# Batch 2's scores in two 64-row bursts, its u turned by DMA: one batch more on the later batches' path, in an attention and MLP-mixer kernel

## The chip, the cores and the metric

The kernel runs on one core of a Trainium2 chip. The metric is the device time of one execution in microseconds (us). A program orders the work of five engines: TensorE (PE, matmuls and their weight loads), VectorE (DVE), ScalarE (ACT), GpSimd (POOL) and SyncE (SP, which only issues DMAs here). Each engine works through its own list of instructions in order; between engines there are semaphores.

## The reference

Eight batches, eight heads, 576 positions, 64 numbers per head. Heads 0 to 3 attend to the last 32 positions, heads 4 to 7 to every fourth of the last 128. The result is a 576 x 512 matrix per batch, which an MLP mixer treats first across positions (token mix) and then across channels.

```python
rel = pos[:, None] - pos[None, :]
mask_plain = (rel >= 0) & (rel < window)                     # window 32, heads 0..3
mask_dil = (rel >= 0) & (rel < window * dilation) & (rel % dilation == 0)   # dilation 4, heads 4..7
attn = softmax(where(mask, q @ k.T / 8, -1e9))
x = (attn @ v), heads side by side                           # [8, 576, 512]
xt = x.transpose(0, 2, 1)
u = x + (np.maximum(xt @ w_tok1, 0.0) @ w_tok2).transpose(0, 2, 1)
out = u + np.maximum(u @ w_ch1, 0.0) @ w_ch2                 # 512 -> 1536 -> 512
```

## The kernel before, in words

**Stages of a batch.** Loads in fp32; casts to fp16 (`cast_steps`, L274, 9 for q, k and tails, 8 for v); q and k turned so that the 64 numbers of a head lie on partitions; scores and their exponentials; masks; `values` (L543), attention weights by v, with a column of ones for the sum, and DVE's reciprocal and product `xn`; the token mix `emit_h1` (L570) and `emit_u` (L581), whose sum with x is u; u turned (`emit_uT`, L607, on TensorE, or `uT_dma` and `uT_place`, L633 and L641, by DMA); and `gen_main` (L695), the channel MLP: twelve blocks `gp` of four 128x512 matmuls with a relu each, in odd batches also three blocks `gt` of the 64-row tails of two batches, then the products `yp` back to 512 channels, 24 matmuls of 256 columns for each quarter of the positions, added to u on DVE and stored.

**The order of the work.** The order is written by hand. `interleave` (L764) runs `gen_main(b)` piece by piece, counting an assumed time, and between the pieces puts the steps of later batches whose time has come: each step is a triple of time, cost and function. In the main part of batch b lie the values and the token mix of batch b+1, the scores and casts of batch b+2, and the loads of batch b+3. The tables of times are at the end of the program (L953 on), with a case of their own for b = 0, for b = 1, and one for all others. A step that issues instructions appends them to several engines' lists at once: a score step gives matmuls to PE, exponentials to ACT and masks to POOL.

**Two ways to make scores.** Batches 0 to 2 (`scores_plain`, `scores_dil`, L420 and L446) use all 128 rows of the array: the keys of two heads lie on 128 partitions, and the queries are copied into `qz`, padded with zeros for the other head. TensorE turns q and k there (`transposes`, L303) into one bank of PSUM per pair of heads. Batches 0 and 1 add a bias (`veil`) by a matmul; batch 2 is masked on POOL as the later ones are. Batches 3 to 7 (`by_dma`, L342) have q, k and tails turned by DMA into `qt`, `kr` and `tt`, unpadded; POOL copies the keys of the plain heads into `kt` (`place_steps`); and `scores_twin` (L465) issues two bursts, g = 0 for the plain heads and g = 1 for the dilated ones, each 24 matmuls over 64 rows, two heads at a time in the two halves of the array. A burst fills six banks: two of the ring `sc` and two of the ring `fl` for the four large tiles, one more of `fl` and one of `main` for the small ones (the last blocks and the tails of the 64 last positions). Behind it come its exponentials on ACT, eight for g = 0 (four of 480 columns, four of 256) and six for g = 1, and three masks on POOL. The ring `fl` has three banks and also serves the transposes, the values and the token mix.

**u.** For b < 3 (`turned`, L630) u is turned by 16 transposes on TensorE and copied out of PSUM by ACT and DVE. For b >= 3 it goes by DMA into `utm`; two of its four blocks are then copied by ACT into `utd`, in the order that `gen_main` wants.

**Start.** `warm(8)` (L779, L836) gives PE eight matmuls on zeros, into a bank that nobody reads, while the first loads travel. The first load of batch 2 waits for the second of three transfers of `w4` (`gate`, L803; q, k and v of batch 2 follow in SP's list). Relus of the gp blocks lie on ACT but for every second one in batch 0 and blocks 1 and 5 in the other batches, which are on DVE; of the three tail relus the first is on DVE.

Of the kernel before, what the change touches and what calls it, by code (L numbers as in the profile page):

```python
# [16 lines left out]
S = 576  # L17
# [51 lines left out]
def kernel(  # L69
# [272 lines left out]
    def by_dma(b):  # L342
        return b >= 3

    def dma_steps(b):

        def turn_over(t, c):
            nc.sync.dma_start_transpose(out=t, in_=c)

        def half(t, nm, i):  # L350
            turn_over(t[:, 2 * i:2 * i + 2].rearrange("p a r m -> p (a r) m"),
                      c16[(b, nm)][:, 2 * i:2 * i + 2].rearrange("m a r h d -> m (a r h d)"))

# [4 lines left out]
        return steps  # L358

    def place_steps(b):  # L360

# [43 lines left out]
    def plain_blocks(hp):  # L405
        return attp[hp].rearrange("p h (b c) -> p h b c", c=PST)
# [58 lines left out]
    def scores_twin(b, g):  # L465

        tags = (("sc", 2), ("sc", 2), ("fl", 3), ("fl", 3), ("fl", 3), ("main", 3))
        ps = [bank(*tags[i], f"sc_{b}_{g}_{i}") for i in range(6)]
        small = ps[4:6]

        def twin(hp, banks, c, keys, queries):
            for h in range(2):
                rows = slice(64 * h, 64 * h + 64)
                n = c.stop - c.start
                nc.tensor.matmul(out=banks[h][:, c], lhsT=keys(rows), rhs=queries(rows), start=True, stop=True)  # L475
# [12 lines left out]
        for j in range(2):  # L488
            hp = 2 * g + j
            if g == 0:  # L490
                twin(hp, small, slice(256 + 128 * j, 384 + 128 * j),
                     lambda rows: kt[hp][rows, 384:512], lambda rows: qta[rows, hp, :, 96:128])
            for x in range(2):
                twin(hp, small, slice(128 * j + 64 * x, 128 * j + 64 * x + 64),
                     lambda rows: kt[hp][rows, 384 + 128 * x:512 + 128 * x], lambda rows: tta[rows, hp, 0:64])
        yield 0.87

        def exp(out, in_):
            nc.scalar.activation(out=out, in_=in_, func=AF.Exp, scale=0.125)  # L499

        def main(hp):
            for h in range(2):
                p = ps[2 * (hp % 2) + h]
                if g == 0:
                    exp(plain_blocks(hp)[:, h, 0:3, 0:BLK].rearrange("p b (m r) -> p b m r", r=4),
                        p[:, 0:3 * BLK].rearrange("p (b r m) -> p b m r", r=4, m=40))
                else:
                    exp(attd[hp - 2][:, h], p)

        def rest():  # L510
            for h in range(2):
                p = small[h]
                if g == 0:
                    exp(attpa[:, :, h, 3 * PST:3 * PST + 128].rearrange("p a (m r) -> p a m r", r=4),
                        p[:, 256:512].rearrange("p (a r m) -> p a m r", a=2, r=4))
                t = attt[:, 2 * g:2 * g + 2, h, 64:TW].rearrange("p a (x c) -> p a x c", c=128)[:, :, :, 0:64]
                exp(t, p[:, 0:256].rearrange("p (a x c) -> p a x c", x=2, c=64))
# [21 lines left out]
        if not g:  # L539
            mask(1)  # L540
        yield 0.0

# [85 lines left out]
        uT[(b, cb)] = (t[:, 128:640], t[:, 0:128]) if odd else (t, None)  # L628

    def turned(b):  # L630
        return b >= 3

    def uT_dma(b, tail):  # L633
        i = b % 2
# [12 lines left out]
            uT[(b, cb)] = (uTd[:, cb - 2], tail)  # L647
            nc.scalar.copy(out=natural(uTd[:, cb - 2]), in_=uTm[i][:, cb].rearrange("p r m -> p m r"))

    def score_steps(b, t0, dt, offs=(0.0, 0.7, 2.0), places=None):  # L650

        steps = []
        if by_dma(b):
            for g in range(2):
                for i, f in enumerate([scores_twin(b, g)] * 2):
                    steps.append((t0 + g * dt, 0.86 * (i == 0), lambda f=f: next(f)))
# [38 lines left out]
    def gen_main(b):  # L695
# [7 lines left out]
        def gp_tails(g):  # L703
            p = bank("main", 3, f"gt_{b}_{g}")
            for i in range(4):
                for cb in order:
                    nc.tensor.matmul(  # L707
                        out=p[:, 128 * i:128 * i + 128], lhsT=w3_block(cb, 4 * g + i), rhs=uT[(b, cb)][1],
                        start=(cb == order[0]), stop=(cb == order[-1]))
            relu(nc.scalar if g else nc.vector, gta[:, 4 * g:4 * g + 4, 512:640],  # L710
                 p.rearrange("p (i t) -> p i t", t=128))

        for mb in range(NMB):
            p = bank("main", 3, f"gp_{b}_{mb}")
            for i, cb in enumerate(order):
                nc.tensor.matmul(out=p, lhsT=w3_block(cb, mb), rhs=uT[(b, cb)][0], start=(i == 0), stop=(i == 3))  # L716
# [236 lines left out]
    for b in range(B):  # L953
        steps = []
        if b == 0:
# [7 lines left out]
            steps += score_steps(2, 0, 0, (0.0, 1.0, 2.6),  # L963
                                 ((31.0, 33.8), (33.0, 0), (0, 0), (0, 0)))[:7]
            steps += at(37.0, 0.0, [lambda: emit_loads_qk(3)])
        elif b == 1:
            late = score_steps(2, -4.3, 2.4, (0.0, 0.7, 1.6))
            va = value_steps(2, 4.2, 1.0)
            steps += late[7:] + va[:4] + [(9.6 + (0.0, 0.8, 2.8, 3.6)[i], c, f) for i, (_, c, f) in enumerate(va[4:])]
            steps += mix_steps(2, 10.8, 14.6, 17.2, 22.2)  # L970
            steps += score_steps(3, 25.2, 4.2) + at(9.0, 0.6, cast_steps(3))
            steps += at(6.0, 0.0, [lambda: load_v(3)]) + at(20.0, 0.9, load_steps(4))
            steps += at(15.0, 0.7, dma_steps(3)) + at(20.6, 0.4, place_steps(3))
        else:
            late = 2.4 * (b % 2)
            if b + 1 < B:
# [37 lines left out]
```

## Time and profile before

| | us |
|---|---|
| median of three runs | 290.72 |
| lowest, highest | 290.5, 291.42 |
| the profiled execution | 292.38 |
| its span, first to last instruction | 290.6 |
| PE busy in it | 279.4 |
| POOL, ACT, DVE busy in it | 165.7, 134.8, 133.3 |

The profiled execution took 1.8 us beside its span. Times within a trace are counted from the span's start. The granted clock is full in every slice of the page. A row of the timeline has start, length, engine, line, operation, what it writes and reads, shape and count; in brackets, the idle time of the engine before it and what ended it. A matmul's length there reaches from its issue to the modelled end of its pipeline, so that successive ones overlap.

### The profile page before, as it was taken

The numbers are of one execution on the slowest core, as the hardware profiler recorded it, in microseconds if no ns is written. First come the engines' busy times: TensorE is split into PE (matmuls) and PEld (weight loads), VectorE is DVE, ScalarE is ACT, GpSimd is POOL, SyncE is SP. The second block draws the span as 40 slices with busy tenths as digits, with TensorE's granted clock in tenths as the row PEclk, the third lists the DMA queues.
The fourth block names the chain that finished last, engine by engine and source line by source line (L and its number), as shares of the span: only waits on it lengthen the run. The fifth ranks groups of instructions, "written<-read, shape, count | busy, mean of one in ns | idle before, by whom it ended". The sixth has DMA issues, their size and how long they took to land.

```text
span 290.6 us, 7078 instructions
## 1 busy us (share of the span) xinstructions
PE 279.4 (96%) x2850; PEld 214.5 (74%) x2850; DVE 133.3 (46%) x279; ACT 134.8 (46%) x266; POOL 165.7 (57%) x227
## 2 busy tenths in 40 slices
PE   5799999999999999999999999999999999999995
PEld 2687676898676886688676986697776966896594
DVE  6677668456734237413741255415640264422022
ACT  2764673247564703565347615482356525224500
POOL 6980860475996499739962998469952930000000
PEclk9999999999999999999999999999999999999999
DMA  7999998993999986769896989399974220431023
GB/s 215 274 205 260 267 215 165 318 227 95 304 211 204 325 241 151 87 120 346 213 204 137 324 203 219 74 219 333 193 144 97 88 74 2 86 114 38 2 73 108
DMA packets 103472, 52.11 MB, mean 179 GB/s; under 512 B 71792, under 2 KB 102384, under 8 KB 103440
## 3 DMA queue, kind: packets, MB, share of 16 engines
q1 hardware_dynamic: 99200, 46.55, 65.5%
q0 software_dynamic: 2640, 3.94, 7.8%
q10 hardware_dynamic: 1600, 1.18, 1.4%
q8 instruction: 22, 0.36, 0.5%
q14 instruction: 10, 0.08, 0.1%
HBM read 37.07 MB, written 9.44 MB: 160 GB/s over the span
## 4 chain that ended last, share of the span: by engine, by line
PE 65%; ACT 0%; DVE 0%; issue 0%
PE yp L735 25%; PE gp L716 21%; PE h1p L578 3%; PE up L590 3%; PE gt L707 3%; PE yp L755 3%; PE sc L475 2%; PE h1p L576 1%; PE av L554 1%; PE av L559 1%; PE up L601 1%; PE av L552 1%; PE yq L735 0%; PE av L564 0%; PE av L562 0%; ACT h L106 0%
## 5 line engine op out<-in xcount | busy, mean ns | idle before, releaser
L735 PE MATMUL yp<-w,gt 128*128 128x256 f16 x756 | 87.4, 273 | 0.0
L735 PEld LDWEIGHTS <-gt 128*128 128x128 f16 x768 | 78.5, 106 | 6.3
L106 ACT ACTIVATE gt<-gp 128x512 f16<-128x512 f32 x76 | 45.4, 597 | 81.1 <-PE gp L716 80.6
L716 PEld LDWEIGHTS <-w 128*128 128x128 f16 x384 | 39.0, 114 | 19.6 <-issue 0.5
L745 DVE TENSOR_TENSOR o<-yp,u 128x512 f32<-128x512 f32 x31 | 21.4, 691 | 64.2 <-PE yp L735 58.3
L112 POOL TENSOR_TENSOR attp<-attp,const 128x1280 f16<-128x1280 f16 x12 | 31.4, 2613 | 32.1 <-ACT attp L499 28.5
L716 PE MATMUL gp<-utd,w 128*128 128x512 f16 x120 | 45.6, 380 | 0.0
L716 PE MATMUL gp<-utm,w 128*128 128x512 f16 x120 | 45.5, 379 | 0.0
L716 PE MATMUL gp<-uT,w 128*128 128x512 f16 x144 | 38.7, 379 | 0.0
L112 DVE TENSOR_TENSOR xn<-av,rec 128x320 f16<-128x320 f32 x64 | 31.4, 491 | 2.2
L112 POOL TENSOR_TENSOR attd<-attd,const 128x1024 f16<-128x1024 f16 x12 | 25.3, 2132 | 0.0
L596 DVE TENSOR_TENSOR u<-up,xn 128x512 f16<-128x512 f32 x26 | 17.9, 690 | 8.5 <-PE up L590 8.5
L102 POOL CAST c_q<-l_q 128x512 f16<-128x512 f32 x31 | 19.4, 631 | 3.9 <-DMA l_q<-in_q_dram 2.2
L102 POOL CAST c_k<-l_k 128x512 f16<-128x512 f32 x29 | 17.8, 617 | 2.0 <-PE up L590 1.0
L106 ACT ACTIVATE h<-h1p 128x256 f16<-128x256 f32 x29 | 11.1, 383 | 15.9 <-PE h1p L578 15.7
L567 DVE RECIPROCAL rec<-av 128x5 f32<-128x5 f32 x64 | 12.1, 189 | 13.0 <-PE av L564 12.8
L108 DVE TENSOR_SCALAR gt<-gp 128x512 f16<-128x512 f32 x20 | 13.7, 685 | 7.5 <-PE gp L716 7.1
L392 PEld LDWEIGHTS <-kt 128*128 128x128 f16 x144 | 12.4, 105 | 5.1 <-DVE kt L314 2.6
L366 POOL COPY kt<-kr 128x512 f16<-128x512 f16 x10 | 10.8, 1076 | 9.1 <-DMA kr<-c_k 9.1
L499 ACT ACTIVATE attp<-sc 128x480 f16<-128x480 f32 (+1 forms) x30 | 13.4, 528 | 3.0 <-PE sc L475 3.0
L112 POOL TENSOR_TENSOR attt<-attt,const 128x512 f16<-128x512 f16 (+1 forms) x14 | 14.3, 1019 | 0.0
L605 DVE TENSOR_TENSOR u16t<-up,xn 64x512 f16<-64x512 f32 x7 | 4.8, 689 | 19.6 <-PE up L601 19.6
(136 smaller groups left out, 483.3 us busy)
## 6 DMA issues: line engine op xcount, KB each, us to landing
out_dram<-o SPq DMA_DIRECT2D x72, 128.0 KB, 3.0
l_q<-in_q_dram SPq DMA_DIRECT2D x15, 512.0 KB, 6.1
l_k<-in_k_dram SPq DMA_DIRECT2D x14, 512.0 KB, 7.1
l_vn<-in_v_dram SPq DMA_DIRECT2D x32, 128.0 KB, 6.3
l_vd<-in_v_dram SPq DMA_DIRECT2D x16, 256.0 KB, 5.2
w<-in_moe_w_ch_dram POOLq DMA_DIRECT2D x6, 512.0 KB, 7.6
lt<-in_q_dram SPq DMA_DIRECT2D x8, 128.0 KB, 3.7
l_vt<-in_v_dram SPq DMA_DIRECT2D x8, 128.0 KB, 5.4
```

Source lines behind the costliest of these rows:

```text
L102: eng.tensor_copy(out=out, in_=in_)
L106: nc.scalar.activation(out=out, in_=in_, func=AF.Relu)
L108: eng.tensor_scalar_max(out=out, in0=in_, scalar1=0.0)
L112: eng.tensor_tensor(out=out, in0=x, in1=y, op=ALU.mult)
L366: nc.gpsimd.tensor_copy(out=natural(kt[hp][:, 0:512]), in_=kra[:, hp].rearrange("p r m -> p m r"))
L392: nc.tensor.matmul(out=out, lhsT=lhsT, rhs=qz[hp][:, h, queries], start=hide is None, stop=True)
L499: nc.scalar.activation(out=out, in_=in_, func=AF.Exp, scale=0.125)
L567: nc.vector.reciprocal(out=rec[:, :, 0], in_=av[:, :, 64])
L596: nc.vector.tensor_tensor(out=u16(b, s), in0=blocks4(p), in1=blocks4(xn[b][:, s]), op=ALU.add)
L716: nc.tensor.matmul(out=p, lhsT=w3_block(cb, mb), rhs=uT[(b, cb)][0], start=(i == 0), stop=(i == 3))
L735: nc.tensor.matmul(out=p[:, c], lhsT=gta[:, mb, a0:m0 + 512:4] if half else gta[:, mb, a0:a0 + 128], rhs=w4[mb][:, c], start=(mb == 0), st ...
L745: nc.vector.tensor_tensor(out=blocks4(o32), in0=blocks4(p), in1=u16(b, s), op=ALU.add)
```

## The change

It does the following.

- Batch 2 uses `scores_twin` (`twinned`, b >= 2). As its data don't come by DMA, `bare_steps` turns tails, q and k on TensorE, without padding: one tile of four tail transposes (copied by DVE into `kt` and by ACT into `tt`), then per pair of heads a tile of q (copied by ACT into `qt`) and one of k (copied by DVE into `kt`, for the dilated heads into `kr` and a part into `kt`). The first five of these nine steps, the first burst, its exponentials and the other four steps lie in b = 0's main part, the second burst near the beginning of b = 1's.
- In all twins, of batches 2 to 7, the exponentials come in another order: the small tile of the ring `main` first, the four large ones, the small tile of the ring `fl` last. They are steps of their own. The masks stay in their order.
- Batch 2's u is turned by DMA (`turned`, b >= 2).
- In b = 1's main part nine of twelve relus are on DVE; batch 3's casts of q are on ACT; batch 2's values and mix and batch 3's scores come at later times (28.0 and 32.4 for the two bursts, 25.2 and 29.4 before); batch 4's loads too.
- All tail relus are on ACT.
- Nine warming matmuls instead of eight, and three more behind the first transposes.
- The first load of batch 2 waits for the first transfer of `w4` instead of the second.

```diff
+    def twinned(b):
+        return b >= 2
...
+    def bare_steps(b):
+
+        def tails():
+            p = bank("fl", 3, f"tp_t_{b}", FP16)
+            for hp in range(4):
+                nc.tensor.transpose(
+                    out=p[:, 128 * hp:128 * hp + 128],
+                    in_=c16[(b, "t")][:, 2 * hp:2 * hp + 2, :].rearrange("m h d -> m (h d)"), identity=ident)
+            t = p[:, 0:512].rearrange("p (x c) -> p x c", c=128)
+            nc.vector.tensor_copy(out=kta[:, :, 512:S], in_=t[:, :, 64:128])
+            nc.scalar.copy(out=tta, in_=t)
+
+        def turn_over(nm, hp):
+            p = bank("fl", 3, f"tp_{nm}_{b}_{hp}", FP16)
+            for r in range(4):
+                nc.tensor.transpose(
+                    out=p[:, 128 * r:128 * r + 128],
+                    in_=c16[(b, nm)][:, hp, r].rearrange("m h d -> m (h d)"), identity=ident)
+            grid = p[:, 0:512].rearrange("p (r m) -> p r m", r=4)
+            if nm == "q":
+                nc.scalar.copy(out=qta[:, hp], in_=grid)
+            elif hp < 2:
+                nc.vector.tensor_copy(out=natural(kt[hp][:, 0:512]), in_=grid.rearrange("p r m -> p m r"))
+            else:
+                nc.vector.tensor_copy(out=kra[:, hp], in_=grid)
+                nc.vector.tensor_copy(out=natural(kt[hp][:, 384:512]),
+                                      in_=grid[:, :, 96:128].rearrange("p r m -> p m r"))
...
-        main(2 * g)
-        if g:
-            mask(2)
-        main(2 * g + 1)
-        if g:
-            mask(3)
-        rest()
-        if not g:
+        yield from small_exps(1)
+        for hp in (2 * g, 2 * g + 1):
+            for h in range(2):
+                main(hp, h)
+                if g and h:
+                    mask(hp)
+                yield 0.0
+        yield from small_exps(0)
+        if g == 0:
             mask(0)
...
     def turned(b):
-        return b >= 3
+        return b >= 2
...
-            relu(nc.scalar if g else nc.vector, gta[:, 4 * g:4 * g + 4, 512:640],
+            relu(nc.scalar, gta[:, 4 * g:4 * g + 4, 512:640],
...
-            relu(nc.vector if (mb % 2 == 1 if b == 0 else mb in (1, 5)) else nc.scalar, gta[:, mb, m0:m0 + 512], p)
+            relu(nc.vector if (mb % 2 == 1 if b == 0 else mb % 4 != 3 if b == 1 else mb in (1, 5)) else nc.scalar, gta[:, mb, m0:m0 + 512], p)
...
-    warm(8)
+    warm(9)
...
     tp(0)
+    warm(3)
...
-    gate(l32[(2, "t")][0:1, 0, 0:1], w4[4][0:1, 0:1])
+    gate(l32[(2, "t")][0:1, 0, 0:1], w4[0][0:1, 0:1])
...
+            scores2 = score_steps(2, 33.2, 4.4, lag=0.2)
...
-            steps += score_steps(3, 25.2, 4.2) + at(9.0, 0.6, cast_steps(3))
+            steps += score_steps(3, 28.0, 4.4)
```

How the order moves at three places. The first is PE's list around batch 2's second transposes of k (`tp_k_2_1`; `sc_2_0` are the plain heads' score tiles, `yp_0_3` the last quarter of batch 0's output). Before:

```order
L392 MATMUL sc_2_0_0_1233<-qz_64,kt_65 128x160
L309 LDWEIGHTS c_k_2_1081
L309 MATMUL tp_k_2_1_1238<-const_61,c_k_2_1081 128x128
...
L735 LDWEIGHTS gt_93
L735 MATMUL yp_0_3_1225<-w4_87,gt_93 128x256
...
L392 LDWEIGHTS kt_65
L392 MATMUL sc_2_0_1_1250<-qz_64,kt_65 128x160
```

And now:

```order
L777 MATMUL yp_0_2_1156<-w4_87,gt_93 128x256
L378 LDWEIGHTS c_k_2_1086
L378 MATMUL tp_k_2_1_1222<-const_61,c_k_2_1086 128x128
...
L508 LDWEIGHTS kt_65
L508 MATMUL sc_2_0_0_1228<-qt_66,kt_65 128x160
...
L508 MATMUL sc_2_0_1_1229<-qt_66,kt_65 128x160
```

Before, single score groups stand between runs of six yp; now all 24 score matmuls follow the four transposes of k directly, one whole output quarter earlier in the list of yp.

The second is ACT's list from the end of batch 3's second burst on (`attd` and `attt` are weights of the dilated heads and of the tails, `gt_93<-gp_2_0` the first relu of batch 2's main part). Before:

```order
L499 ACTIVATE attd1_75<-sc_3_1_3_1841 128x512
L499 ACTIVATE attt_76<-sc_3_1_4_1842 128x2x2x64
L499 ACTIVATE attt_76<-sc_3_1_5_1843 128x2x2x64
L106 ACTIVATE gt_93<-gp_2_0_1969 128x512
L106 ACTIVATE gt_93<-gp_2_2_2023 128x512
```

And now:

```order
L532 ACTIVATE attt_76<-sc_3_0_4_1807 128x2x2x64
L532 ACTIVATE attt_76<-sc_3_1_5_1889 128x2x2x64
L532 ACTIVATE attd0_74<-sc_3_1_0_1884 128x512
...
L532 ACTIVATE attd1_75<-sc_3_1_3_1887 128x512
L532 ACTIVATE attt_76<-sc_3_1_4_1888 128x2x2x64
L687 COPY utd_92<-utm0_89 128x512 x2
L106 ACTIVATE gt_93<-gp_2_0_1944 128x512
```

The two copies of batch 2's turned u now stand between the exponentials and the relus.

The third is PE's list from batch 3's first burst (`sc_3_0`) on. Before, the burst's last matmul is followed by the whole of `yp_1_0` (the first quarter of batch 1's output) and the three quarters behind it:

```order
L475 MATMUL sc_3_0_5_1764<-tt_68,kt_65 128x64
L735 LDWEIGHTS gt_93
L735 MATMUL yp_1_0_1806<-w4_87,gt_93 128x256
...
L735 MATMUL yp_1_1_1878<-w4_87,gt_93 128x256
...
L735 MATMUL yp_1_2_1909<-w4_87,gt_93 128x256
...
L735 MATMUL yp_1_3_1938<-w4_87,gt_93 128x256
```

And now:

```order
L508 MATMUL sc_3_0_5_1808<-tt_68,kt_65 128x64
L777 LDWEIGHTS gt_93
L777 MATMUL yp_1_2_1795<-w4_87,gt_93 128x256
...
L777 MATMUL yp_1_3_1869<-w4_87,gt_93 128x256
...
L508 MATMUL sc_3_1_0_1884<-qt_66,kr_67 128x128
```

Before, all four quarters (96 matmuls) followed the burst; now 18 of the third and the whole fourth do, 42. The second burst lies among them in both.

More of the change, by code (lines that the diff above doesn't have):

```diff
@@ L358, in dma_steps @@
         return steps
+    def bare_steps(b):
[23 more added lines that the diff above has]
+                                      in_=grid[:, :, 96:128].rearrange("p r m -> p m r"))
+        return [tails] + [lambda nm=nm, hp=hp: turn_over(nm, hp) for hp in range(4) for nm in ("q", "k")]
     def place_steps(b):
@@ L499, in exp, with main, last_blocks, tails @@
             nc.scalar.activation(out=out, in_=in_, func=AF.Exp, scale=0.125)
[L501 to L517, printed above, removed]
+        def main(hp, h):
+            p = ps[2 * (hp % 2) + h]
+            if g == 0:
+                exp(plain_blocks(hp)[:, h, 0:3, 0:BLK].rearrange("p b (m r) -> p b m r", r=4),
+                    p[:, 0:3 * BLK].rearrange("p (b r m) -> p b m r", r=4, m=40))
+            else:
+                exp(attd[hp - 2][:, h], p)
+        def last_blocks(h):
+            exp(attpa[:, :, h, 3 * PST:3 * PST + 128].rearrange("p a (m r) -> p a m r", r=4),
+                small[h][:, 256:512].rearrange("p (a r m) -> p a m r", a=2, r=4))
+        def tails(h):
+            t = attt[:, 2 * g:2 * g + 2, h, 64:TW].rearrange("p a (x c) -> p a x c", c=128)[:, :, :, 0:64]
+            exp(t, small[h][:, 0:256].rearrange("p (a x c) -> p a x c", x=2, c=64))
         def mask(hp):
@@ L525, in mask, with small_exps @@
                 mult(nc.gpsimd, w, w, band[:, :, :, 0:128])
-        main(2 * g)
-        if g:
-            mask(2)
-        main(2 * g + 1)
-        if g:
-            mask(3)
-        rest()
-        if not g:
+        def small_exps(h):
+            if g == 0:
+                last_blocks(h)
+                yield 0.0
+            tails(h)
+            yield 0.0
+        yield from small_exps(1)
[4 more added lines that the diff above has]
+                    mask(hp)
+                yield 0.0
+        yield from small_exps(0)
+        if g == 0:
             mask(0)
@@ L538, in scores_twin @@
         mult(nc.gpsimd, t, t, tails_seen[g])
-        if not g:
+        if g == 0:
             mask(1)
@@ L648, in uT_place, with score_steps @@
             nc.scalar.copy(out=natural(uTd[:, cb - 2]), in_=uTm[i][:, cb].rearrange("p r m -> p m r"))
-    def score_steps(b, t0, dt, offs=(0.0, 0.7, 2.0), places=None):
+    def score_steps(b, t0, dt, offs=(0.0, 0.7, 2.0), places=None, lag=0.0):
         steps = []
-        if by_dma(b):
+        if twinned(b):
             for g in range(2):
-                for i, f in enumerate([scores_twin(b, g)] * 2):
-                    steps.append((t0 + g * dt, 0.86 * (i == 0), lambda f=f: next(f)))
+                f = scores_twin(b, g)
+                at = t0 + g * dt
+                steps.append((at, 0.86, lambda f=f: next(f)))
+                for i in range(7 if g else 9):
+                    steps.append((at + lag * (i + 1), 0.0, lambda f=f: next(f)))
             return steps
@@ L962 @@
             steps += at(24.0, 0.5, casts)
[L963 to L964 removed]
+            bare = bare_steps(2)
+            scores2 = score_steps(2, 33.2, 4.4, lag=0.2)
+            scores2 = sorted(scores2, key=lambda st: st[0])
+            steps += [(t, 0.25, f) for t, f in zip((30.2, 30.8, 31.4, 32.0, 32.6, 35.1, 35.5, 35.9, 36.3), bare)]
+            steps += scores2[:10]
             steps += at(37.0, 0.0, [lambda: emit_loads_qk(3)])
         elif b == 1:
[L967 to L970, printed above, removed]
[L971 to L973 removed]
+            va = value_steps(2, 7.0, 1.0)
+            steps += [(1.4 + 0.5 * i, c, f) for i, (_, c, f) in enumerate(scores2[10:])]
+            steps += va[:4] + [(13.4 + 0.9 * i, c, f) for i, (_, c, f) in enumerate(va[4:])]
+            steps += mix_steps(2, 12.4, 17.4, 20.4, 32.6)
+            casts = cast_steps(3)
+            steps += [(10.0 + 0.6 * i, 0.0, casts[i]) for i in (0, 2, 4, 6, 8)]
+            steps += [(10.0 + 1.2 * i, 0.0, lambda i=i: cast_qk(3, "q", i, nc.scalar)) for i in range(4)]
+            steps += at(17.0, 0.3, casts[9:])
+            steps += score_steps(3, 28.0, 4.4)
+            steps += at(6.0, 0.0, [lambda: load_v(3)]) + at(22.0, 0.9, load_steps(4))
+            steps += at(16.0, 0.7, dma_steps(3)) + at(20.6, 0.4, place_steps(3))
         else:
```

## The prediction

> **What bounds the kernel now.** I read the page's busy times first, then the timeline of TensorE (PE), then, at each place where the change puts something else, the timelines of ScalarE (ACT), VectorE (DVE) and GpSimd (POOL), and last the chain of waits.
>
> ```profile
> PE 279.4 (96%) x2850; PEld 214.5 (74%) x2850; DVE 133.3 (46%) x279; ACT 134.8 (46%) x266; POOL 165.7 (57%) x227
> ```
>
> PE is the bound on average: the other engines have 40% and more to spare. So the time changes by the PE work that is removed, and by the stalls of PE that come or go. Columns in what follows: start in us, length, engine, line, what; in brackets the idle time before it and its releaser. Lengths on PE are from issue to end, so I take the distance of starts as the cost of matmuls.
>
> Three landmarks: 61.45, where batch 1's third block of u has been transposed (up to there the order is the old one, but for the first 15 us); **T1**, the end of batch 3's first burst of scores (96.14 now); **L**, batch 3's first product of head 4 with its tails (112.09 now). Behind L the order is again the old one.
>
> ```profile
> 61.45 0.82 PE L735 MATMUL yp<-w,gt 128*128 128x256 f16 x6
> 65.13 0.37 PE L392 MATMUL sc<-qz,kt 128*128 128x160 f16 x3
> 65.33 0.39 PE L309 MATMUL tp_k<-const,c_k 128*128 128x128 f16 x4
> 65.56 0.82 PE L735 MATMUL yp<-w,gt 128*128 128x256 f16 x6
> 67.73 0.39 PE L392 MATMUL sm<-qz,kt 128*128 128x128 f16 x6
> 67.96 1.03 PE L716 MATMUL gp<-uT,w 128*128 128x512 f16 x4
> 71.98 0.39 PE L392 MATMUL sc<-qz,kt 128*128 128x128 f16 x4
> 72.20 0.39 PE L309 MATMUL tp_k<-const,c_k 128*128 128x128 f16 x4
> 75.20 0.20 PE L562 MATMUL av<-vv,attt 128*128 128x65 f16 x1 [0.24 <-POOL attt L112]
> ...
> 91.43 0.23 PE L624 MATMUL tpu<-const,u 128*128 128x128 f16 x1 [0.19 <-DVE u L596]
> ...
> 95.81 0.23 PE L475 MATMUL sc<-qt,kt 64*128 64x128 f16 x2 [0.37 <-DVE uT L102]
> 96.14 2.79 PE L735 MATMUL yp<-w,gt 128*128 128x256 f16 x24
> ...
> 99.54 8.04 PE L735 MATMUL yp<-w,gt 128*128 128x256 f16 x72
> 107.41 0.59 PE L716 MATMUL gp<-uT,w 128*128 128x512 f16 x2
> 112.09 0.19 PE L562 MATMUL av<-vt,attt 128*128 128x65 f16 x1
> ```
>
> The bracketed rows are the long waits of the old order here. Counted from issue to issue they are .41, .35 and .55, and gaps under .2 add about .5: 1.8 us that the old order loses between 61.45 and T1, and nothing from T1 to L.
>
> **Work taken off PE.** Batch 2's scores are four groups of 3 matmuls (65.13 to 65.33, .20), two of 6 (67.73 to 67.96, .23), four of 4 (71.98 to 72.20, .22), and two of four half as wide, which I estimate at .11: 2.36 us. The two bursts take their place:
>
> ```profile
> 124.80 0.75 PE sc L475 x24
> 128.93 0.67 PE sc L475 x24
> ```
>
> That is batch 4's pair, 1.42 us: .94 saved. The transposes of q and k stay on PE, with the tails in a tile of their own. Batch 2's u loses 16 transposes at .058 (four in .23, 65.33 to 65.56): .9. Together **-1.8**. The old stalls, which hung on that u and on the masks and scores at their old places, go too: **-1.8**.
>
> **New stalls before T1.**
>
> ```profile
> 61.65 0.69 ACT L100 COPY uT<-tpu 128x640 f16<-128x640 f16 x1 [1.18 <-PE tpu L626]
> ```
> ```profile
> 65.76 0.69 DVE L314 COPY kt<-tp_k 128x512 f16<-128x512 f16 x1 [0.60 <-PE tp_k L309]
> ```
> ```profile
> 95.33 2.23 ACT L499 ACTIVATE attp<-sc 128x480 f16<-128x480 f32 x5 [0.87 <-PE sc L475]
> 97.40 0.43 ACT L499 ACTIVATE attt<-sc 128x256 f16<-128x256 f32 x1
> 97.67 0.45 ACT L499 ACTIVATE attp<-sc 128x256 f16<-128x256 f32 x1
> 99.36 2.06 ACT L499 ACTIVATE attd<-sc 128x512 f16<-128x512 f32 x4 [0.97 <-PE sc L475]
> 101.28 0.69 ACT L499 ACTIVATE attt<-sc 128x256 f16<-128x256 f32 x2
> 131.80 2.13 ACT L648 COPY utd<-utm 128x512 f16<-128x512 f16 x2
> ```
>
> (1) Batch 1's last block of u now comes eight transposes (.44) after 61.45, in the PSUM bank that ACT copies out from 61.65 to 62.34; 61.89 becomes 62.40: .5. (2) The first burst stands right behind the last k transposes. DVE starts on such a copy .20 after them (65.56, 65.76), takes .69, and a PE waiting for it starts some .06 later: .95, of which six matmuls of the burst hide .20: .75. (3) The burst uses all three banks of the transposes' ring. Twelve yp (1.31) lie behind it, then q2, k2, q3, k3 want those banks back. ACT can begin .20 after the burst's end T, takes the small exps of the other bank first (2 x .27, 97.40 to 97.67), then the mains at .45 (95.33 to 97.40 holds four and one small). The third main ends near T+2.2, while PE is ready at T+1.3: .9; the next three banks cost .23, .41 and .21 in the same way: 1.8. (4) The token mix comes a little ahead of the last normalization on DVE, which now has nine of batch 1's twelve relus: .3, between 0 and 1. Sum **+3.4**; the lower end is 0 if the banks come free sooner than the exps' row says, the upper 4.5.
>
> **From T1 to L.** This is the main term. Now 96 yp (24 and 72) follow T1; in the new order 42 do, since batch 3's bursts stand 54 matmuls later. A yp costs .1093 (99.54 to 107.41 is 72 of them). PE's own work there is 42 x .1093 = 4.59, the second burst .67 and, from 107.41 to 112.09, 4.68: 9.94. Against it stands POOL, which masks what ACT has exponentiated:
>
> ```profile
> 98.26 2.61 POOL L112 TENSOR_TENSOR attp<-attp,const 128x1280 f16<-128x1280 f16 x1 [4.91 <-ACT attp L499]
> ...
> 108.69 1.15 POOL L112 TENSOR_TENSOR attt<-attt,const 128x512 f16<-128x512 f16 x1
> ```
>
> The masks run without a gap from 98.26 to 109.84: 11.58. In the new order the first one needs the last exp but one: T1 + .20 + 2 x .27 + 4 x .45 + .45, and .14 to POOL (97.67+.45 to 98.26) = T1 + 3.13. So L can't come before T1 + 14.71, and with .06 it is T1 + 14.77. PE is ready at T1 + 9.94: **+4.8** of stall. Now the masks end 2.25 ahead of L, so there it costs nothing. Part of the 4.8 is met sooner: the first gp of batch 2 waits for the copy of its turned u (131.80: two in 2.13), queued on ACT behind all exps of both bursts. The second burst ends at T1 + 3.95, its exps follow from T1 + 4.15 (.27, four at .48 by 99.36 to 101.28, .27), and the first copy ends near T1 + 7.7, where PE stood ready at T1 + 5.3. These 2.5 are inside the 4.8, not beside it.
>
> Sum: -1.8 - 1.8 + 3.4 + 4.8 = **+4.6** from 61.45 to L.
>
> **Start.** The warming matmuls are the part that can gain.
>
> ```profile
> 2.54 3.60 PE L783 MATMUL idle_p<-idle 128*128 128x512 f16 x8 [2.54 <-POOL idle L160]
> 6.77 0.59 PE L309 MATMUL tp_q<-const,c_q 128*128 128x128 f16 x4 [0.64 <-DMA const<-consts]
> ...
> 8.57 0.32 PE L392 MATMUL sc<-qz,kt 128*128 128x160 f16 x1 [0.65 <-ACT qz L100]
> ...
> 10.02 0.63 PE L309 MATMUL tp_q<-const,c_q 128*128 128x128 f16 x4
> 10.44 0.63 PE L309 MATMUL tp_k<-const,c_k 128*128 128x128 f16 x4
> ...
> 11.86 0.24 PE L392 MATMUL sc<-qz,kt 128*128 128x160 f16 x1 [0.24 <-DVE kt L314]
> ...
> 14.62 0.40 PE L309 MATMUL tp_k<-const,c_k 128*128 128x128 f16 x4 [0.68 <-DVE c_k L102]
> ```
> ```profile
> 8.43 0.52 DVE L102 CAST c_k<-l_k 128x512 f16<-128x512 f32 x1
> 11.11 0.69 DVE L314 COPY kt<-tp_k 128x512 f16<-128x512 f16 x1 [2.16 <-PE tp_k L309]
> ...
> 12.56 2.00 DVE L102 CAST c_k<-l_k 128x512 f16<-128x512 f32 x1
> ```
>
> Four transposes cost .42 at 10.02 and .23 at 65.33: PE runs at half rate until about 11, though it has worked since 2.54, with idle pieces of .64 and .65 between. One warming matmul more goes into the first, three into the second. If the full rate then comes near 8.5, the 1.45 from 8.57 to 10.02 and the .85 of the next eight transposes halve, DVE's copy at 11.11 comes 1.1 sooner, and the cast behind it, whose end PE awaits at 14.62, by up to as much; that cast takes 2.00 where the one on DVE at 8.43 takes .52, so a luckier place could give another 1.5. Bounds: -2.5 to +.5 (four matmuls at .45 by the row at 2.54, less the 1.29 that was idle). Batch 1's casts on POOL later absorb some. I take **-1.2**, half of the gain's end, since PE and DVE share the chain.
>
> The Trainium skill ("TensorE: Matmul & The Clock Gate", Part 1) says that the array is at half rate by default, goes to full after a busy window of some 3.4 us that runs freely, and so at a moment that varies from run to run. The rows agree on the half rate; that idle pieces of .64 kept the window from counting is not shown. By the rule alone the gain may be there in one run and not in another, which is the rival "cold start" below.
>
> **Edits with one answer.** Queries cast on ACT rather than POOL, batch 2's loads released by an earlier weight transfer, tail relus on ACT: taken as 0. They lie on engines at 46 to 57% while PE is the bound. The new order of exps delays the first mask of the later batches by .54 (two small exps):
>
> ```profile
> 138.56 1.16 POOL L112 TENSOR_TENSOR attt<-attt,const 128x512 f16<-128x512 f16 x1
> ```
> ```profile
> 140.79 0.19 PE L562 MATMUL av<-vt,attt 128*128 128x65 f16 x1
> ```
>
> Batch 4's masks end 139.72, 1.07 ahead of their use: .5 stays.
>
> **The number.** +4.6 - 1.2 = +3.4. The profiled execution lasted 292.38 us (span 290.6 and 1.8 around it); its like would be 295.8. It is 1.7 above the median of 290.72, so I forecast 290.72 + 3.4 = 294.1. About .3%, .87 us, is what can be told from no change.
>
> **Rivals.**
> - *Cold start.* The rate comes no sooner: the start gives 0 to +.5, and the sum is +4.6 to +5.1: 295.4. For it: PE was awake 8 us in vain. Against: the idle is there to be filled. Chance .22.
> - *The stalls before T1 don't come, the masks bind.* If ACT and DVE return the banks in time, T1 is 3.4 sooner: +1.2 without the start, 0.0 with it: 290.8 to 291.9. For it: the bank order is worked out by hand. Chance .12.
> - *Faster: the masks don't bind either.* If POOL's chain from T1 took less than 9.94, PE's work alone would decide: -1.8 - 1.8 - 1.2 and what is left of 3.4, that is -1.4 to -4.8; 288.5. It decides where 11.58 of masks fall below 6.8, so half of the first burst's masks must have been done earlier than I place them. Against it: they can't start before the burst. Chance .06. A start gain of 2.5 together with the second rival gives 289.5: .06.
> - *Worse: the loss carries on.* The 1.07 of batches 4 and 6 is used up because POOL goes behind L later by 2 us with casts, and each loses up to 1; or a stall of 2.5 us puts PE at half rate again, some 3 us at double cost, +1.5. No row shows a stall above .68 after 12 us. 297. Chance .07.
>
> The forecast keeps .47; its own range, with half to all of the 3.4 and the start from 0 to -2, is 292.0 to 295.3. From 290.2 to 296.0 leaves out most of the third rival and the last. Faster .12: the third and its neighbour; same .09: most of the second; slower .79.
>
> **What would show it.** Right: batch 3's first masks start about 3.1 behind the burst, PE waits for POOL at head 4's tails and for ACT's copy at batch 2's first gp, 4 to 5 us together; and three to four waits near 62 to 70 for ACT and DVE. The start: four transposes in .23 before 10. Wrong: PE without idle between T1 and L, or batch 3's burst near its old time.

## The result and the profile after

| | us |
|---|---|
| before, median of 4 (lowest, highest) | 290.61 (290.38, 291.42) |
| changed, median of 4 (lowest, highest) | 295.88 (295.08, 297.13) |
| ratio, 95% interval | 1.0163, 1.0129 to 1.0197 |
| profiled execution of the changed kernel, its span | 295.08, 293.2 |
| profiled execution of before, its span | 292.38, 290.6 |

The change costs 5.3 us by the medians, 4.7 by the ratio (3.7 to 5.7 by its interval). The two profiled executions differ by 2.7 only, and that is itself a finding: the one of before was 1.8 us slower than its median (experiments b0 and w1), and the one of the changed kernel was the fastest of its four.

The page of the changed kernel: busy times, and the row of the granted clock in 40 slices.

```profile
PE 279.2 (95%) x2838; PEld 211.8 (72%) x2838; DVE 132.5 (45%) x277; ACT 134.6 (46%) x266; POOL 163.3 (56%) x221
...
PEclk9999999999999998999999999999999999999999
```

PE is busy about as long as before in a span that is longer, although work was taken off; and one slice, the sixteenth (110 to 117 us), has a clock below the rest. TensorE's list of waits (what waited, for whom, us in total, how often, the longest):

```profile
PE gp L758 <- ACT utd L687: 3.3, 1, 3.3
...
PE tp_q L378 <- ACT attp L532: 0.8, 1, 0.8
...
PE sc L508 <- DVE kt L385: 0.5, 1, 0.5
...
PE tpu L654 <- ACT uT L100: 0.3, 1, 0.3
```

All four are new, and all four are waits that the prediction named. Here they are on TensorE's timeline, first those before batch 3's first burst. The place that was 61.45 is 59.64 now.

```profile
59.64 0.39 PE L368 MATMUL tp_t<-const,c_t 128*128 128x128 f16 x4
59.87 0.39 PE L378 MATMUL tp_q<-const,c_q 128*128 128x128 f16 x4
60.59 0.38 PE L654 MATMUL tpu<-const,u 128*128 128x128 f16 x4 [0.33 <-ACT uT L100]
...
62.94 0.38 PE L508 MATMUL sc<-qt,kt 64*128 64x160 f16 x6
63.79 0.44 PE L508 MATMUL sc<-qt,kt 64*128 64x160 f16 x8 [0.47 <-DVE kt L385]
...
64.33 1.50 PE L777 MATMUL yp<-w,gt 128*128 128x256 f16 x12
66.63 0.38 PE L378 MATMUL tp_q<-const,c_q 128*128 128x128 f16 x4 [0.79 <-ACT attp L532]
67.09 0.38 PE L378 MATMUL tp_k<-const,c_k 128*128 128x128 f16 x4
67.64 0.38 PE L378 MATMUL tp_q<-const,c_q 128*128 128x128 f16 x4 [0.17 <-ACT attt L532]
68.12 0.38 PE L378 MATMUL tp_k<-const,c_k 128*128 128x128 f16 x4
68.34 2.13 PE L777 MATMUL yp<-w,gt 128*128 128x256 f16 x18
```

Bracketed idle times are short because the pipeline still drains; counted from issue to issue, the last block of u comes .50 late (60.09 to 60.59), the second half of the burst .6, and the four late transposes, .22 each when nothing holds them, take from 65.64 (12 yp behind 64.33) to 68.34: 1.8 of waiting. Now the boundary between batches 1 and 2, on TensorE, ScalarE, GpSimd and SyncE:

```profile
100.00 3.45 PE L777 MATMUL yp<-w,gt 128*128 128x256 f16 x30
...
104.05 1.50 PE L777 MATMUL yp<-w,gt 128*128 128x256 f16 x12
108.84 0.38 PE L758 MATMUL gp<-utd,w 128*128 128x512 f16 x1 [3.29 <-ACT utd L687]
...
110.28 0.63 PE L758 MATMUL gp<-utm,w 128*128 128x512 f16 x1
110.71 0.63 PE L758 MATMUL gp<-utd,w 128*128 128x512 f16 x1
111.14 0.63 PE L758 MATMUL gp<-utm,w 128*128 128x512 f16 x1
...
115.16 0.19 PE L601 MATMUL av<-vt,attt 128*128 128x65 f16 x1
```
```profile
106.41 0.43 ACT L532 ACTIVATE attt<-sc 128x256 f16<-128x256 f32 x1
107.73 2.04 ACT L687 COPY utd<-utm 128x512 f16<-128x512 f16 x2 [0.89 <-DMA utm<-u]
```
```profile
103.14 2.61 POOL L112 TENSOR_TENSOR attp<-attp,const 128x1280 f16<-128x1280 f16 x1 [11.98 <-ACT attp L532]
...
113.54 1.16 POOL L112 TENSOR_TENSOR attt<-attt,const 128x512 f16<-128x512 f16 x1
```
```profile
97.89 0.68 SPq L190 DMA_DIRECT2D l_q<-in_q_dram  x1
98.66 5.54 SPq L677 DMA_TRANSPOSE utm<-u  x1
104.25 0.58 SPq L190 DMA_DIRECT2D l_k<-in_k_dram  x1
```

T1 is 100.00 and L 115.16, so 15.16 lie between, with 9.94 of work. The first mask starts 3.14 behind T1 (forecast 3.13) and the last ends at 114.70 (forecast 114.71). But the masks are not what TensorE waits for: the first gp of batch 2 waits longer than forecast, since the DMA that turns u, issued at 98.66 among batch 4's loads, needs until 107.71, 9.0 us where its kind has a median of 4.4. And behind that wait TensorE runs at half rate: gp matmuls stand .43 apart (110.28, 110.71, 111.14), not .216. The window from that wait on, by engine, with the granted clock as the third number from the end:

```profile
108.84:112.50 3.66, 3.66 (x26) 1.96 (x26) 0.88 (x3) 1.53 (x2) 3.66 (x3) 0.55 0.88 221
```

3.66 us at .55 lose 1.65 (the half rate itself begins at about 109.2 and lasts 3.4 us). With these the masks are overtaken, by .4 us.

### The profile page after: what moved, and what is told of

It is laid out like the page before. It is cut to its first block, busy times and chain, and to the rows that moved or that the text cites. A ratio compares the mean times of both kernels' runs of the same rounds, so it can differ in the third digit from the quotient of the medians.

```text
span 293.2 us, 7001 instructions
## 1 busy us (share of the span) xinstructions
PE 279.2 (95%) x2838; PEld 211.8 (72%) x2838; DVE 132.5 (45%) x277; ACT 134.6 (46%) x266; POOL 163.3 (56%) x221
## 4 chain that ended last, share of the span: by engine, by line
PE 85%; DMA 5%; DVE 4%; ACT 3%; POOL 2%; issue 1%; SPq 0%; ACTq 0%; POOLq 0%
PE gp L758 27%; PE yp L777 26%; PE h1p L617 4%; PE up L629 4%; PE gt L749 4%; PE yp L797 3%; DMA utm<-u 3%; PE sc L508 2%; DVE xn L112 2%; DMA l_q<-in_q_dram 2%; PE h1p L615 1%; PE av L593 1%; PE sc L423 1%; PE sc L425 1%; PE av L598 1%; PE up L640 1%
## 5 line engine op out<-in xcount | busy, mean ns | idle before, releaser
L106 ACT ACTIVATE gt<-gp 128x512 f16<-128x512 f32 x69 | 41.2, 597 | 71.5 <-PE gp L758 71.2
L758 PE MATMUL gp<-utd,w 128*128 128x512 f16 x144 | 55.4, 385 | 3.3 <-ACT utd L687 3.3
L758 PE MATMUL gp<-utm,w 128*128 128x512 f16 x144 | 55.3, 384 | 0.0
L108 DVE TENSOR_SCALAR gt<-gp 128x512 f16<-128x512 f32 x27 | 18.6, 688 | 13.8 <-PE gp L758 13.3
L758 PE MATMUL gp<-uT,w 128*128 128x512 f16 x96 | 24.8, 380 | 0.0
L532 ACT ACTIVATE attp<-sc 128x480 f16<-128x480 f32 (+1 forms) x36 | 15.8, 535 | 15.3 <-PE sc L508 15.3
L102 POOL CAST c_q<-l_q 128x512 f16<-128x512 f32 x27 | 16.9, 630 | 3.5 <-DMA l_q<-in_q_dram 3.5
L687 ACT COPY utd<-utm 128x512 f16<-128x512 f16 x12 | 12.6, 1115 | 4.9 <-DMA utm<-u 4.9
L532 ACT ACTIVATE attt<-sc 128x256 f16<-128x256 f32 x24 | 9.8, 409 | 9.8 <-PE sc L508 9.8
L112 POOL TENSOR_TENSOR attt<-attt,const 128x512 f16<-128x512 f16 x12 | 13.9, 1160 | 0.0
```

Of the source, the lines that this page charges most:

```text
L102: eng.tensor_copy(out=out, in_=in_)
L112: eng.tensor_tensor(out=out, in0=x, in1=y, op=ALU.mult)
```

## The experiments

Each kernel was timed beside the kernel before on the same chip; that one's median lay at 291.28 to 291.40 in these rounds. Diffs of the tables of times show only the terms of a line that changed.

**b0: the kernel before, once more.**

> The kernel before, once more, for its start and its span. Theory 'lucky start': the rate of TensorE comes at a moment that varies, and the profiled execution of before (292.38 us, 1.8 above the median) had a late one (four transposes in .42 us at 10.0); most executions have an early one. Then this profile probably shows four transposes in about .23 us before 10 us and a span of about 288.8. Theory 'filled start': only the added warming brings the rate early. Then this profile looks like the first: half rate until 11 us, and the difference between 292.4 and the median lies elsewhere.

Ratio 1.0004 (0.998 to 1.0028), profiled execution 291.18 us with a span of 289.4. Its start on TensorE and VectorE:

```profile
6.68 0.38 PE L309 MATMUL tp_q<-const,c_q 128*128 128x128 f16 x4 [0.54 <-DMA const<-consts]
...
8.84 0.39 PE L309 MATMUL tp_q<-const,c_q 128*128 128x128 f16 x4
9.06 0.39 PE L309 MATMUL tp_k<-const,c_k 128*128 128x128 f16 x4
```
```profile
11.44 1.02 DVE L102 CAST c_k<-l_k 128x512 f16<-128x512 f32 x1
```

Four transposes take .22 at 8.84, with the old eight warming matmuls and the old idle piece of .54. In the first profile they took .42 at 10.02. VectorE's cast that took 2.00 there takes 1.02 here. The place of 61.45 is 60.26 here. The 23 runs of before that were timed beside this one fall in two groups, 14 from 290.27 to 291.67 and 9 from 292.25 to 293.04: their medians lie 1.3 apart, near the 1.2 us by which the place of 61.45 differs in the two profiles. That the groups are the two starts is read from the times; only two of before's executions left a profile, and in a later round of 18 the gap between the groups is filled. With w1 below, "lucky start" holds. The granted clock doesn't show the half rate of the start: it is 1.00 from 8.5 to 11.9 in the first profile, and 1.000 over the run in all nine of the upper group. There the spacing of the matmuls has to be read.

**w1: the added warming alone, on the kernel before.**

```diff
-    warm(8)
+    warm(9)
...
     tp(0)
+    warm(3)
```

> The kernel before with the nine and three warming matmuls alone. 'Filled start': 1.5 to 2 us faster than before in the median (about 288.9). 'Lucky start': within .5 us of before in the median, since most executions of before have the early rate already; the profile shows the early rate in any case.

Ratio 0.9982 (0.9963 to 1.0001): .5 us faster, at most 1.1. Its twelve runs lie between 290.74 and 291.62; none is in the upper group. So the warming takes away the bad draws, which are some 4 in 10, and leaves the good ones as they are (medians 291.05 with the warming, 291.14 in the lower group of before).

**a_nowarm: the changed kernel with the old warming.** The diff is the reverse of w1's.

> The changed kernel with eight warming matmuls and none behind the first transposes, as before. 'Filled start': 1.5 to 2 us slower than the changed kernel (about 297.6). 'Lucky start': about the changed kernel's 295.9, with more spread.

Ratio 1.0172 (1.013 to 1.0213) against 1.0163 of the changed kernel, six runs from 294.99 to 298.61. Its profile drew the late start:

```profile
9.85 0.63 PE L309 MATMUL tp_q<-const,c_q 128*128 128x128 f16 x4
10.28 0.63 PE L309 MATMUL tp_k<-const,c_k 128*128 128x128 f16 x4
```

The median is .55 above the changed kernel's, with more spread, nearer to "lucky start" than to "filled start". The spread isn't the start's alone: the two slowest executions (297.06 and 298.61) have a mean clock of .988, the others .994.

**a_uPE: batch 2's u by TensorE again.**

```diff
     def turned(b):
-        return b >= 2
+        return b >= 3
```

> The changed kernel, but batch 2's u turned by TensorE as before, all else and all times kept. The wait of 3.3 us for the turned u at batch 2's first gp goes, and the half rate behind it. Theory 'masks next': GpSimd's masks end 14.7 us behind batch 3's first burst whatever u does, so the wait moves to head 4's products, L stays about 14.8 behind T1 (15.2 now) and the time falls by at most .5 us, to 295.4, or rises if the new wait of 4 us brings a half rate of its own. Theory 'only u': the turned u alone held TensorE, L comes 10.9 behind T1, and the time falls by 4 us, to 291.6.

Ratio 1.0136 (1.0104 to 1.0167), 295.39 us: .5 less in the median than the changed kernel's 295.88, within either's interval. T1 and what follows on TensorE:

```profile
100.70 3.45 PE L777 MATMUL yp<-w,gt 128*128 128x256 f16 x30
...
106.85 0.38 PE L663 MATMUL tpu<-const,u 128*128 128x128 f16 x4 [2.03 <-ACT attd L532]
...
115.46 0.20 PE L601 MATMUL av<-vt,attt 128*128 128x65 f16 x1 [1.16 <-POOL attt L112]
```

L is 14.76 behind T1; the masks were forecast to hold it at 14.77. The wait for the turned u is gone, and two others have come: the transposes wait for a bank that holds the second burst's scores, and head 4's tails for the mask. "Only u" (10.9) is out. The profile is at full clock (.999); the other five executions have .994, so some half rate came back in those, at a place that isn't known.

**a_loads: batch 4's loads later.**

```diff
-at(22.0, 0.9, load_steps(4))
+at(28.0, 0.9, load_steps(4))
```

The time is 28.0, not the 29.0 that the expectation names.

> The changed kernel with batch 4's loads issued later (29.0 instead of 22.0 in b = 1's table), so that the DMA that turns batch 2's u doesn't stand among them. In the changed kernel it took 9.0 us to landing (98.66 to 107.71), the median of its kind is 4.4. Theory 'three in a row' (the DMA, ScalarE's exps and copies, GpSimd's masks each hold batch 2's start, the last of them decides): the DMA lands near 103, the wait at the first gp falls from 3.3 to about 2.6, then the masks hold L at 14.8 behind T1: .4 us less than the changed kernel, and the half rate behind the wait is shorter or gone. Theory 'the DMA alone': the wait goes nearly whole, L 11 to 12 behind T1, 3 us less.

Ratio 1.0129 (1.0096 to 1.0162), 294.96 us.

```profile
99.99 3.45 PE L777 MATMUL yp<-w,gt 128*128 128x256 f16 x30
...
107.82 0.38 PE L758 MATMUL gp<-utd,w 128*128 128x512 f16 x1 [2.28 <-ACT utd L687]
...
114.76 0.20 PE L601 MATMUL av<-vt,attt 128*128 128x65 f16 x1 [1.82 <-POOL attt L112]
```

Three in a row, as expected: the DMA, now ahead of batch 4's loads, lands 4.4 behind its issue and is early enough, the first gp comes 7.83 behind T1, held by ScalarE's queue of exps (forecast in the prediction: the first copy ends near T1 + 7.7), and L 14.77 behind T1, held by the masks. This profile ran at full clock throughout (the other three executions have .993 or .994), and its span is .4 shorter, as forecast; the medians differ by .9, and the intervals of the two ratios overlap.

**a_bound: batch 3's bursts earlier as well.** First burst ahead of the last products of the token mix, second 7.0 later; the step that places keys moved ahead of it.

```diff
-steps += mix_steps(2, 12.4, 17.4, 20.4, 32.6)
+steps += mix_steps(2, 12.4, 17.4, 23.6, 32.6, 0.7)
-steps += score_steps(3, 28.0, 4.4)
+steps += score_steps(3, 20.8, 7.0)
-at(22.0, 0.9, load_steps(4))
+at(29.0, 0.9, load_steps(4))
-at(20.6, 0.4, place_steps(3))
+at(19.0, 0.3, place_steps(3))
```

> As a_loads, and batch 3's first burst about 8 us earlier in the list (ahead of the token mix's last products; second burst 7.0 behind it, keys placed before). All three then lie beside yp matmuls. My theory: waits and half rate at the boundary go, 3.5 + 1.7 = 5.2 us less than the changed kernel: 290.7, level with before (ratio 0.998 to 1.003), since the three waits of 62 to 70 remain. Rival 'some other edit costs it': the boundary's waits go but the time stays 2 us or more above before.

Ratio 1.0174 (1.0128 to 1.0219): no gain. The boundary's waits are gone, but one of its own came, in TensorE's list of waits:

```profile
PE sc L508 <- POOL kt L399: 3.7, 2, 2.9
```

Batch 4's first burst waits for its keys, since batch 4's loads now come too late. My edit, not one of the change's, put it there, so the time tests neither theory. But the trace up to L does:

```profile
59.24 0.39 PE L368 MATMUL tp_t<-const,c_t 128*128 128x128 f16 x4
...
110.03 0.19 PE L601 MATMUL av<-vt,attt 128*128 128x65 f16 x1
```

From the place of 61.45 to L it needs 50.79 us, 4.73 less than the changed kernel and .15 more than before. The boundary's stall is bought back by moving the bursts, nearly as my theory has it (5.2).

**a_gap: batch 2's transposes and bursts spread.** One yp run of six more ahead of the first burst, 18 instead of 12 behind it, three of the late transposes between batch 1's first gp, the second burst 2.5 later.

```diff
-scores2 = score_steps(2, 33.2, 4.4, lag=0.2)
+scores2 = score_steps(2, 33.8, 4.4, lag=0.2)
...
-(30.2, 30.8, 31.4, 32.0, 32.6, 35.1, 35.5, 35.9, 36.3)
+(29.6, 30.6, 31.6, 31.6, 32.8, 36.6)
...
-(1.4 + 0.5 * i, c, f)
+(0.4 + 0.6 * i, 0.25, f) for i, f in enumerate(bare[6:])
+(3.9 + 0.5 * i, c, f)
```

> The changed kernel with batch 2's transposes spread: the tails ahead of batch 1's last u block but one, the first burst six yp behind the last k of the plain heads, the last q behind 18 yp, the other three between batch 1's first gp, the second burst 2.5 later. My theory: the three waits of 62 to 70 (.4, .6 and 1.8) go and nothing replaces them: T1 2.8 us earlier, 293.1. Rival 'given back': VectorE's copies and relus, and GpSimd's masks of batch 2, come later by as much and batch 2's products wait for them: less than 1 us gained.

Ratio 1.0095 (1.006 to 1.0129), 294.14 us: some 2 us less than the changed kernel. In its profile the three waits have .34, 0 and .15 in brackets instead of .33, .47 and .96, and a new one of .37 stands at batch 2's first product of values. The wait at the first gp is still there, 3.6 in brackets where the changed kernel has 3.3. So these waits are worth 2, not 2.8; most of the gain is kept, and "given back" (less than 1) is out.

**best: a_bound and a_gap together.**

> a_bound and a_gap together. My theory: the terms add, 8 us less than the changed kernel, 3 less than before: 288.0 (ratio 0.990). What is left of the change is then the 1.8 us of work taken off TensorE, the old waits of 1.8, and the steadier start. Rival: what the masks and copies gain at one place they lose at another: no better than before.

Ratio 1.0039 (1.0007 to 1.007), 292.15 us, twelve runs from 290.65 to 294.70. The same fault as in a_bound: batch 4's keys wait for loads, on GpSimd's timeline and in the windows behind it.

```profile
122.62 1.04 POOL L399 COPY kt<-kr 128x512 f16<-128x512 f16 x1 [2.25 <-DMA kr<-c_k]
```
```profile
125.00:128.00 3.00, 2.96 (x28) 2.29 (x29) 0.00 (x0) 1.80 (x5) 0.74 (x2) 0.50 0.89 166
```

My theory's .990 is missed. The granted clock is .50 from 125 to 128: half rate again, behind waits of 2.2 and .7 on TensorE. Here it lasts 6.8 us, from 123.8 to 130.6, twice as long as in the changed kernel. Of the twelve runs six kept a mean clock of 1.000 and took 290.65 to 291.86; the six with .994 or .988 took 292.43 to 294.70. Only the slowest of the twelve left a profile, so the waits of the others aren't known.

**a_bound2, best2: the loads ahead of the u DMA.** As a_bound and best, with `at(19.2, 0.4, load_steps(4))`.

> a_bound with batch 4's loads issued early (19.2 in b = 1's table, ahead of the u DMA) instead of late; the late loads had made batch 4's first burst wait 3.7 us for keys and cost a half rate there. My theory: no wait above .5 us is left behind 68, 5.2 us less than the changed kernel, level with before (ratio 0.998 to 1.004); the three waits of 62 to 70 remain. Rival: the u DMA lands after 104 behind those loads and a wait of 1 to 3 us at the first gp of batch 2 comes back.

> a_bound2 and a_gap together: a further 2.8 us, ratio to before 0.988 to 0.994, about 288.3 where before is 291.3. Rival: as for a_bound2, or what a_gap gains is lost at a later wait: ratio 0.997 or more.

Ratios 1.0291 (1.0255 to 1.0327) and 1.0219 (1.0175 to 1.0264), worse than anything else here. The rival holds, with longer waits than its 1 to 3 us. a_bound2 on SyncE and on TensorE:

```profile
96.36 5.75 SPq L207 DMA_DIRECT2D l_vn<-in_v_dram  x4
...
106.88 3.06 SPq L677 DMA_TRANSPOSE utm<-u  x1
```
```profile
113.00 0.58 PE L758 MATMUL gp<-utd,w 128*128 128x512 f16 x1 [7.08 <-ACT utd L687]
```

Four issues of batch 4's v take 5.75 us of SyncE's queue, and the u DMA is issued at 106.88, some 8 us later than in the changed kernel; the first gp waits 7.1 (4.8 in best2).

**best3: the loads directly behind it.** As best, with `at(27.9, 0.2, load_steps(4))`.

> As best2, but the loads issued in one row directly behind the u DMA. My theory: u lands by 102, the loads by about 108; GpSimd's casts of batch 4 wait some 1 us for them and its keys are placed just in time: as best2 within .5 us. Rival: the loads are too late again, batch 4's first burst waits 1 us or more, 290 or above.

Ratio 1.0112 (1.0071 to 1.0154): the rival again. Batch 4's first burst waits 1.98 and .94 for keys.

**best4: u by TensorE, the loads at their old place.** As best, with `turned` from batch 3 on, `at(20.0, 0.9, load_steps(4))`, the bursts at 21.2 and 28.0, the token mix's u at 24.0 and its transposes at 31.6.

> a_bound and a_gap together, but batch 2's u turned by TensorE again and batch 4's loads where they stood before (20.0). The last three runs showed that the u DMA and batch 4's loads can't both be in time in the one queue that SyncE issues; so this one leaves the DMA out and pays .9 us of transposes. My theory: no wait above .6 us behind 60, no half rate; against before .9 us less work and some 1.5 of old waits gone: 2 us faster, ratio 0.990 to 0.996. Rival 'no room': the transposes wait for banks behind the second burst's exps, or keys of batch 4 are late again by 1 us or more: ratio 0.998 or above, and the twin for batch 2 brings nothing whatever stands around it.

Ratio 0.9955 (0.9939 to 0.9972): 290.13 us, 1.3 less than before, the only kernel here whose whole interval lies below 1. All that is left of TensorE's waits behind 60 and above .3:

```profile
PE av L593 <- ACT attd L532: 0.4, 1, 0.4
PE tpu L654 <- ACT tt L373: 0.3, 1, 0.3
PE sc L508 <- POOL kt L399: 0.3, 1, 0.3
```

```profile
60.88 0.39 PE L378 MATMUL tp_q<-const,c_q 128*128 128x128 f16 x4
...
110.87 0.19 PE L601 MATMUL av<-vt,attt 128*128 128x65 f16 x1
```

From the place of 61.45 to L it needs 49.99, and .22 more for the four transposes of the tails, which stand ahead of that place here: 50.21. Before needed 50.64 and 50.66 in its two profiles, the changed kernel 55.52. Its clock is full in the profile. The ratio is at the upper end of what I expected; how much of it is the warming (w1: 0.9982) wasn't taken apart.

## Why the prediction was right, and where it was not

- **Work taken off, old stalls gone (-1.8, -1.8), new stalls (+3.4).** Before T1 the changed kernel needs 40.36 us from the place of 61.45 (59.64 to 100.00), before 34.69. 54 yp moved ahead of T1 make 5.90 of that, so all the rest adds up to -.23; forecast was -.2. Of the new stalls, .5, .75 and 1.8 were forecast and .5, .6 and 1.8 are there; the fourth, .3 for the last normalization, isn't, since TensorE's idle time from 70.31 to 100.00 is .14 in all. a_gap gives 2 us back when these are spread. Right in sum, with some luck: the new stalls came about .5 short of the forecast, so the work and the old stalls must have saved about 3.1, not 3.6.
- **From T1 to L (+4.8).** 15.16 were needed instead of 14.77. The masks' chain was right to .01 (T1 + 14.70), and a_loads and a_uPE put L at 14.77 and 14.76 when the rest is out of the way. But in the changed kernel itself the masks only came second, and its trace has no wait for POOL at head 4's tails, one of the signs that the prediction named. The step that failed here is "the first copy ends near T1 + 7.7": it counted ScalarE's queue and left out the u DMA itself, with the queue that it stands in. That DMA took 9.0 us (4.4 in a_loads, ahead of the loads), the first gp came 8.84 behind T1, and the half rate behind that wait added what the masks would otherwise have taken.
- **The half rate.** It was in the text as part of the rival "worse", at +1.5, with the remark that no row showed a stall long enough. It costs 1.65 in the profile, and all four executions have the same mean clock of .994, but it hardly shows in the sum, as the masks would have held L nearly as long. By the Trainium skill ("TensorE: Matmul & The Clock Gate", Part 1) the array falls to half rate after an idle window of some 3.4 us that runs freely. The spell of 3.4 us fits that figure. The wait is 3.48 from issue to issue (105.36 to 108.84), but the clock falls only at about 109.2, and in the 3.4 us before that TensorE had worked in some .3; best's profile has half rate behind waits of 2.2 and .7. So a wholly idle window isn't needed here, and the runs decide; what share of a window is enough stays open.
- **Start (-1.2).** Wrong as a term of the median. The step took the profiled execution of before as its median's like, though it lay 1.7 above. It had drawn the late rate, which is 1.2 of that 1.7 (b0); 14 of 23 executions, by their times, draw the early one without any added matmul. What the warming is worth in the mean is .5 (w1, between 0 and 1.1), by taking away the bad draws. The rival "cold start" had the right size, 295.4, for another reason.
- **Edits at 0, and what is behind L.** 178.04 us from L to the end, before 178.51 and 178.48. Batch 4's masks end at 143.27 and are wanted at 143.85: .6 of slack, forecast .5. Right.
- **The sum.** With the start taken at 0 to -.5 the forecast would have been 294.8 to 295.3; 295.88 was measured. Against b0's profile, which has an early start as well, the changed kernel's span is 3.8 longer: 4.86 up to L, .44 less behind it, .62 less at the start. The other three executions of the changed kernel took .75 to 2.05 more than the profiled one; where they lost it stays open, as they left no trace.

## What to carry to other kernels

A step moved on the bottleneck engine moves a whole chain: scores moved 54 matmuls later took exponentials, masks and a copy out from under the matmuls that had covered them, and the longest chain behind the moved step (here 14.8 us) has to be set against the bottleneck's own work up to its user (9.9). Work taken off the bottleneck by a DMA must be paid for in that DMA's queue: with u, loads and stores in one queue, none of the orders tried here had both u and the loads in time once batch 3's bursts stood earlier (ahead of u, behind it, directly behind it), and giving the 16 transposes back to TensorE was the cheaper way. And before a term is read from one profile, set that execution against the median: before's profile lay 1.7 us above the median, and 1.2 of that were a late start, not a cost.

## What the runs showed of the hardware

- TensorE's full rate was there at 6.7 us in one profile of the kernel before and came between 11.3 and 11.9 in the other, with idle pieces of .54 and .64 us behind the same eight warming matmuls; by their times, 14 of 23 executions had the early one, and with four more warming matmuls twelve of twelve.
- Half rate came back in the middle of a kernel in every profile with a wait above 2.9 us in brackets, behind waits of 2.2 and .7 (best) and 2.0 and .9 (best3) too, but not behind 2.3 and, 7 us later, 1.8 (a_loads) or 2.0 and 1.2 (a_uPE). By the granted clock a spell lasts 3.4 us (the changed kernel, a_nowarm, a_gap, best3) or 6.8 (a_bound, best, a_bound2, best2), which is a mean clock of .994 or .988 over 293 us. Of the 70 executions of before in the later rounds three have .993 or .994, at 291.1 to 292.2 us; where it came in those isn't known.
- One DMA that turns a 128 x 2048 tile took 4.4 us to landing in the median and 9.0 behind three loads of 512 KB, and held SyncE's queue for 5.5; ahead of those loads it held the queue for 1.9 (a_loads).
